# Attention and routed experts on one core: values as products of 64 rows without zeros, and x of four batches held back

## The chip, the cores and the metric

The kernel runs on one core of a Trainium2 chip. The metric is the device time of one execution in microseconds (us); lower is better. PE is TensorE's matmul, PEld its weight load, DVE is VectorE, ACT ScalarE, POOL GpSimd, and SP the engine that issues most of the plain transfers.

## The reference

```python
def _attn_ref(q, k, v, g_norm):              # (8, 8, 576, 64) each, g_norm (64,)
    kv = np.einsum('bhsd,bhse->bhde', k, v)
    out = np.einsum('bhsd,bhde->bhse', q, kv)
    rms = np.sqrt(np.mean(out * out, axis=-1, keepdims=True) + 1e-06)
    return out / rms * g_norm

# x = attention's output as (4608, 512)
def _moe_ref(x, w_skip, w_gate, w1, w2):     # 8 experts: w1 (8, 512, 1024), w2 (8, 1024, 512)
    do_compute = x @ w_skip > 0
    xc = x[do_compute]
    logits = xc @ w_gate
    e_idx = np.argmax(logits, axis=1)
    probs = np.exp(logits - logits.max(-1, keepdims=True))
    probs /= probs.sum(-1, keepdims=True) + 1e-09
    gate_w = probs[np.arange(len(xc)), e_idx]
    for e in range(E):
        mask = e_idx == e
        h = np.maximum(xc[mask] @ w1[e], 0.0)
        y[mask] = gate_w[mask, None] * (h @ w2[e])
    out = x.copy()
    out[do_compute] = xc + y
```

Everything is in fp32.

## The kernel before

Two stages follow each other: attention (to about 127 us of the profiled span), then the eight experts on rows gathered by an indirect transfer.

**Attention** works batch by batch, with eight heads of 64 each. Two heads share an operand: `w` numbers the two head pairs of a half, `u` the two halves of the heads, and `r` or `a` the two heads or rows of a pair, so that a head fills 64 of the 128 rows. For each batch six parts make the state, the product of k and v:

- `state` (L343), in thirds: 64x64 products of k and v into `sum_ps`; after the last third ACT copies the sums into `kvd` (L350).
- `state_t` (L357): the state turned, into `kvT_ps`, and copied by ACT (L360).
- `state_m` (L366): the turned state times the gate weights. The result gives nine more columns per head, so that a product of q with the state yields the gate logits beside the values; ACT copies them to both ends of the state (L369).
- `state_s` (L375, L379): the rows of the two heads of a pair swapped, through `sw_ps`, and copied by ACT.

`kvd` is a ring of five tiles (`KVD = 5`). In the kernel before, a tile is a block diagonal of 128 rows: each half of the rows holds its own state and zeros beside it, written once by memsets (L316: tile 0 by DVE, the others by POOL). Its values are then products over all 128 rows with 146 columns that move:

```python
nc.tensor.matmul(out=ps[:, w, 0:2 * PK].rearrange("p (r k) -> p r k", r=2)[:, :, cols],
                 lhsT=qT[:, w, a, :], rhs=kvds[b % KVD][:, u, w, :, cols], ...)
```

The work is cut into 36 **units**: four for each batch (two quarters `i` times two halves `u`), and after every four batches two more, with `i` None, for the ninth row of each group (L458, 64x64 products). Batch b of the first four starts at unit 4b, batches 4 to 7 at units 18, 22, 26 and 30. A unit takes these steps, pipelined over the loop `for n in range(NU + 2)`: `turn` (L414, four transposes of q, and ACT's copy L417), `values` (L450, into a tile of `ps_o`, of which there are two, or late in the stage into `sum_ps`), ACT's squares (L464), `squares` (DVE's sum L472), `root` (ACT L479), `norm` (DVE's reciprocal L486 and the product `xl` L489, which empties the PSUM tile), and `finish` (POOL: the logits L506 to L514 and the product with g_norm into `xb`, L524).

The order on every engine is the order of the program[...]. Jobs for a later step are put in lists by `at(step, part, job)` and called at the parts "early", "pe", "dve" and "end" of that step. The state of batch b is made at the steps from six before its first unit on. At the end of its first unit `load_kv(b + 3)` is issued on SP (there are three buffers each for k and v), and two steps later `load_q(b + 2)` (two buffers). When a batch's `xb` is done, one half is stored by POOL's queue (L545) and the other, one step later, by SP's (L546).

The gating runs beside it in three groups (`ends = [12, 22, 36]`): from steps 12 and 22 on, a few DVE operations a step choose, rank and number the rows of the tokens so far. In the second group the order of the experts is found, the weights of the first one are loaded on SP (L302, L305, into the tiles `w1` and `w2` of `wpool_a`), and `early` gathers the first 128 rows of that expert from the batches 0 to 4 already stored (L756).

**Experts.** The first expert's layers are plain products (L972, L983), the other seven use products of half-size blocks and sums (L1051). The weights of each next expert are loaded while the one before runs.

## Time and profile before

| What | Value |
|---|---|
| Median of 3 runs | 403.25 us (401.68 to 403.75) |
| Profiled execution, its own time | 404.02 us |
| Its span | 402.2 us |
| Busy: PE, PEld, DVE, ACT, POOL | 371.8, 323.1, 254.4, 144.7, 123.5 us |
| Mean granted clock | 0.956 |
| Read from and written to memory | 66.80 and 14.48 MB |
| Last xl of the attention stage, start | 128.4 us |
| First product of the first expert (L972), start | 129.25 us |

Times in the profile count from the start of the span. A line such as L450 is a line of the kernel before; the changed kernel has other numbers for the same operations. An fp32 matmul of the program is two matmul instructions with a weight load each, while a transpose is one. Matmuls are pipelined, so that the time from the first start of a group to the first start of the next says more than the durations. Busy shares are of the whole span; what a stage is bound by is read from a table of windows.

### The profile page before, as it was taken

The numbers are of one execution on the slowest core, as the hardware profiler recorded it, in microseconds if no ns is written. First come the engines' busy times: TensorE is split into PE (matmuls) and PEld (weight loads), VectorE is DVE, ScalarE is ACT, GpSimd is POOL, SyncE is SP. The second block draws the span as 40 slices with busy tenths as digits, with TensorE's granted clock in tenths as the row PEclk, the third lists the DMA queues.
The fourth block names the chain that finished last, engine by engine and source line by source line (L and its number), as shares of the span: only waits on it lengthen the run. The fifth ranks groups of instructions, "written<-read, shape, count | busy, mean of one in ns | idle before, by whom it ended". The sixth has DMA issues, their size and how long they took to land.

```text
span 402.2 us, 9616 instructions
## 1 busy us (share of the span) xinstructions
PE 371.8 (92%) x3849; PEld 323.1 (80%) x3849; DVE 254.4 (63%) x621; ACT 144.7 (36%) x384; POOL 123.5 (31%) x192
## 2 busy tenths in 40 slices
PE   7789999999874989999999999999999999999992
PEld 4678988888763948859978987998988988989981
DVE  2233568899976761366674775766766776868811
ACT  1365786676743212203510440430430430431410
POOL 7024577665658243111204301231221111212001
PEclk9599999999986898999999999999999999999997
DMA  8999999898595882346252651752752752711001
GB/s 299 394 391 392 316 391 400 250 364 222 169 406 134 255 322 73 102 161 224 73 203 67 250 193 55 260 182 94 257 188 90 258 177 96 255 55 38 16 2 49
DMA packets 31287, 81.70 MB, mean 203 GB/s; under 512 B 1850, under 2 KB 1858, under 8 KB 31236
## 3 DMA queue, kind: packets, MB, share of 16 engines
q1 hardware_dynamic: 26688, 66.59, 47.9%
q0 software_dynamic: 4528, 14.41, 11.0%
q8 instruction: 32, 0.52, 0.5%
q14 instruction: 19, 0.16, 0.1%
q10 hardware_dynamic: 20, 0.02, 0.0%
HBM read 66.80 MB, written 14.48 MB: 202 GB/s over the span
## 4 chain that ended last, share of the span: by engine, by line
PE 71%; DVE 10%; issue 8%; ACT 4%; DMA 3%; POOL 2%; ACTq 0%; DVEq 0%; POOLq 0%
PE bank L1051 40%; PE bank L983 8%; PE bank L972 6%; PE o_ps L450 4%; DVE xl L489 3%; PE sum_ps L343 3%; PE q_ps L414 3%; PE bank L953 2%; DMA xg<-out_dram,src 2%; DVE rs L472 1%; PE g_ps L357 1%; DMA xb<-in_g_norm_dram 1%; ACT qT L417 1%; PE g_ps L366 1%; ACT rs L479 1%
## 5 line engine op out<-in xcount | busy, mean ns | idle before, releaser
L1061 ACT COPY p<-bank 128x144 f32<-128x144 f32 (+4 forms) x70 | 20.9, 299 | 106.1 <-PE bank L1051 91.9
L1051 PE MATMUL bank<-xt,w 128*128 128x144 f32 (+3 forms) x336 | 56.5, 291 | 0.0
L1051 PEld LDWEIGHTS bank<-xt,w 128*128 128x128 f32 x336 | 47.8, 190 | 1.9 <-DVE bank L1055 1.2
L1055 DVE TENSOR_TENSOR bank<-bank,p 128x144 f32<-128x144 f32 (+4 forms) x70 | 23.8, 340 | 40.3 <-PE bank L1051 38.5
L450 PE MATMUL o_ps<-kvd,qT 128*128 128x146 f32 x240 | 36.9, 296 | 3.8 <-DVE xl L489 1.4
L1193 POOL DMA_INDIRECT out_dram<-xg,rows x16 | 16.2, 1011 | 77.8 <-DVE xg L1190 77.2
L524 POOL TENSOR_TENSOR xb<-xl,g_b 128x512 f32<-128x512 f32 x32 | 38.2, 1193 | 1.2 <-DMA out_dram<-xb 1.2
L1051 PE MATMUL bank<-xs,s 128*128 128x144 f32 (+3 forms) x224 | 37.4, 292 | 0.0
L450 PEld LDWEIGHTS o_ps<-kvd,qT 128*128 128x128 f32 x240 | 32.5, 193 | 5.7 <-DVE xl L489 2.4
L983 PE MATMUL bank<-w,ht 128*32 128x128 f32 (+2 forms) x448 | 36.6, 322 | 0.0
L943 POOL DMA_INDIRECT xg<-out_dram,src x15 | 15.9, 1057 | 56.3 <-PE bank L1051 36.2
L1193 POOL DMA_INDIRECT out_dram<-xg,arows x8 | 9.0, 1129 | 76.9 <-DVE xg L1190 76.6
L1051 PEld LDWEIGHTS bank<-xs,s 128*128 128x128 f32 x224 | 31.6, 190 | 1.0 <-ACT p L1061 0.3
L472 DVE TENSOR_REDUCE rs<-sq 128x8 f32<-128x512 f32 x36 | 24.4, 679 | 12.3 <-ACT sq L464 12.1
L983 PEld LDWEIGHTS bank<-w,ht 128*32 128x32 f32 (+2 forms) x448 | 20.4, 121 | 13.6 <-issue 10.9
L489 DVE TENSOR_TENSOR xl<-o_ps,rs 128x584 f32<-128x584 f32 x33 | 25.3, 767 | 4.4 <-PE g_ps L366 0.5
L1051 PE MATMUL bank<-w,ht 128*128 128x256 f32 x112 | 27.2, 386 | 0.0
L1051 PE MATMUL bank<-t,ht 128*128 128x256 f32 x112 | 27.1, 385 | 0.0
L343 PE MATMUL sum_ps<-v,k 64*64 64x64 f32 x1152 | 25.3, 229 | 1.4 <-issue 0.9
L972 PE MATMUL bank<-xt,w 128*128 128x128 f32 (+1 forms) x128 | 24.4, 360 | 1.5 <-ACT xt L956 1.0
L343 PEld LDWEIGHTS sum_ps<-v,k 64*64 64x64 f32 x1152 | 21.7, 140 | 4.5 <-issue 2.6
L1051 PE MATMUL bank<-t,hs 128*128 128x256 f32 x112 | 25.3, 379 | 0.0
(198 smaller groups left out, 697.0 us busy)
## 6 DMA issues: line engine op xcount, KB each, us to landing
w<-in_moe_w_dram SPq DMA_DIRECT2D x16, 2048.0 KB, 10.3
q<-in_q_dram SPq DMA_DIRECT2D x8, 1152.0 KB, 12.0
k<-in_k_dram SPq DMA_DIRECT2D x7, 1152.0 KB, 12.2
v<-in_v_dram SPq DMA_DIRECT2D x7, 1152.0 KB, 14.7
out_dram<-xb SPq DMA_DIRECT2D x8, 512.0 KB, 8.1
out_dram<-xb POOLq DMA_DIRECT2D x8, 512.0 KB, 7.5
k<-in_k_dram SPq DMA_DIRECT2D x2, 576.0 KB, 4.8
v<-in_v_dram SPq DMA_DIRECT2D x2, 576.0 KB, 6.8
```

The lines of the kernel that those rows point to most:

```text
L343: nc.tensor.matmul(out=sum_ps[w * 64:(w + 1) * 64, a, u, :], lhsT=kt[r, 2 * u + w, c, :], rhs=vt[r, 2 * u + w, c, :], start=(c == 0), stop ...
L450: nc.tensor.matmul(out=ps[:, w, 0:2 * PK].rearrange("p (r k) -> p r k", r=2)[:, :, cols], lhsT=qT[:, w, a, :], rhs=kvds[b % KVD][:, u, w, ...
L472: nc.vector.tensor_reduce(out=rs[:, :, :], in_=sq[:, :, :, :].rearrange("p x y (a d) -> p x (y a) d", a=2), axis=AX.X, op=ALU.add)
L489: nc.vector.tensor_tensor(out=xl[:, :, :, :].rearrange("p x y (a k) -> p x (y a) k", a=2), in0=ps[:, :, 0:2 * PK].rearrange("p x (h k) -> ...
L524: late.append(lambda: nc.gpsimd.tensor_tensor(out=xb[:, :, 4 * u * D:(4 * u + 4) * D].rearrange("p r (w x) -> p r w x", w=2), in0=xl[:, :, ...
L943: nc.gpsimd.indirect_dma_start(out=x_of(xg, off, m), out_offset=None, in_=cut_rows(m)[:, :], in_offset=bass.IndirectOffsetOnAxis(ap=idx[:, ...
L972: nc.tensor.matmul(out=hps[:, cols], lhsT=w_sb[r][0][:, dc, f * P:(f + 1) * P], rhs=xt[:, dc, cols], start=(dc == 0), stop=(dc == DC - 1))
L983: nc.tensor.matmul(out=yps[q * m:(q + 1) * m, 0:n], lhsT=ht[:, f, off:off + m], rhs=w_sb[r][1][:, f, q * n:(q + 1) * n], start=(f == 0), s ...
L1051: nc.tensor.matmul(out=out, lhsT=lhsT(i), rhs=rhs(i), start=start and i == 0, stop=i == k - 1, skip_group_check=True)
L1055: nc.vector.tensor_tensor(out=to, in0=x, in1=y, op=ALU.add)
L1061: nc.scalar.copy(out=t, in_=x)
L1193: ins = nc.gpsimd.indirect_dma_start(out=cut_rows(m)[:, :], out_offset=bass.IndirectOffsetOnAxis(ap=rows[:, col:col + 1], axis=0), in_=x, ...
```

## The change

Four things are done together.

1. `kvd` loses its zeros: a tile is `[P, 2, 2, PK]`, the own state and the swapped one, and no memset is left. Values become products of 64 rows: for each `w` and `a`, one for each half `r` of the rows, with 128 columns of weights and 73 columns that move, and the two halves write to different PSUM banks.
2. ACT's copies in `state`, `state_m` and `state_s`, two of 64 partitions each, become one of 128. `state_t` uses two transposes of 128x128 where it had four matmuls with the identity; `state_m` has four matmuls with 64 columns of weights where it had two with 128.
3. x of batches 0 to 3 is written into the room of the tiles `w1` (batches 0, 1) and `w2` (2, 3) of the first expert's weights, and not stored when done. Both halves are stored later by SP's queue, one batch at the end of each of the steps 21 to 24. Batches 4 to 7 are stored as before.
4. `load_kv(b + 3)` is issued at the end of step n - 3, where it was step n, but not before step 3 (batch 0's stays at step 0).

```diff
-        t = kvd_pool.tile([P, 2, 2, 2, PK], FP32, name=f"kvd{i}")
-        for r in range(2):
-            (nc.vector if i < 1 else nc.gpsimd).memset(t[r * 64:(r + 1) * 64, :, :, 1 - r, :], 0.0)
-        kvds.append(t)
+        kvds.append(kvd_pool.tile([P, 2, 2, PK], FP32, name=f"kvd{i}"))
...
-        for w in range(2):
-            nc.scalar.copy(out=own(b, w)[:, :, G:G + 2 * D].rearrange("p u (a d) -> p a u d", a=2),
-                           in_=sum_ps[w * 64:(w + 1) * 64, :, :, :])
+        nc.scalar.copy(
+            out=kvds[b % KVD][:, 0, :, G:G + 2 * D].rearrange("p u (a d) -> p a u d", a=2), in_=sum_ps)
...
     def state_t(b):
         for u in range(2):
-            for w in range(2):
-                r = slice(w * 64, (w + 1) * 64)
-                nc.tensor.matmul(out=kvT_ps[:, u, r], lhsT=kvds[b % KVD][:, u, w, w, G:G + 2 * D],
-                                 rhs=ident[:, r], start=True, stop=True)
+            nc.tensor.transpose(out=kvT_ps[:, u, :], in_=kvds[b % KVD][:, 0, u, G:G + 2 * D],
+                                identity=ident[:, :])
...
     def state_m(b):
...
-            nc.tensor.matmul(out=lg_ps[:, u, :, :, :], lhsT=kvT[:, u, :], rhs=gw_b[:, u, :, :, :],
-                             start=True, stop=True)
-        for w in range(2):
-            nc.scalar.copy(out=ends_of(own(b, w)), in_=lg_ps[w * 64:(w + 1) * 64, :, :, w, :])
+            for w in range(2):
+                r = slice(w * 64, (w + 1) * 64)
+                nc.tensor.matmul(out=lg_ps[r, u, :, :], lhsT=kvT[:, u, r], rhs=gw_b[:, u, :, w, :],
+                                 start=True, stop=True, skip_group_check=True)
+        nc.scalar.copy(out=ends_of(kvds[b % KVD][:, 0, :, :]), in_=lg_ps)
...
     def state_s(b):
...
-        for w in range(2):
-            o = slice((1 - w) * 64, (2 - w) * 64)
-            nc.scalar.copy(out=kvds[b % KVD][o, :, w, 1 - w, :],
-                           in_=sw_ps[o, :].rearrange("p (u k) -> p u k", u=2))
+        nc.scalar.copy(out=kvds[b % KVD][:, 1, :, :].rearrange("p u k -> p (u k)"), in_=sw_ps)
...
     def values(n):
...
-                if i is not None:
-                    nc.tensor.matmul(
-                        out=ps[:, w, 0:2 * PK].rearrange("p (r k) -> p r k", r=2)[:, :, cols],
-                        lhsT=qT[:, w, a, :], rhs=kvds[b % KVD][:, u, w, :, cols],
-                        start=True, stop=True, skip_group_check=True)
-                    continue
...
+                for r in range(2):
+                    rows, to = slice(r * 64, (r + 1) * 64), slice(w * PK + a * KD, w * PK + (a + 1) * KD)
+                    if i is not None:
+                        nc.tensor.matmul(out=ps[:, r, to], lhsT=qT[rows, w, a, :],
+                                         rhs=kvds[b % KVD][rows, w ^ r, u, cols],
+                                         start=True, stop=True, skip_group_check=True)
+                        continue
...
+    HELD = 4
+    stages, held_rows = {}, {}
+
+    def kept(b):
+
+        if b % 2 == 0:
+            shape, tag = ([P, DC, F], "w1") if b < 2 else ([P, FC, DM], "w2")
+            stages[b // 2] = wpool_a.tile(shape, FP32, tag=tag, name=tag)
+        flat = stages[b // 2][:, :, :].rearrange("p c f -> p (c f)")
+        n = NQ * 2 * DM
+        return flat[:, b % 2 * n:(b % 2 + 1) * n].rearrange("p (i r d) -> p i r d", i=NQ, r=2)
+
+    def store_held(b):
+        for hf in range(2):
+            rows, xb = held_rows.pop((b, hf))
+            nc.sync.dma_start(out=rows, in_=xb)
...
-                xbs[b, 0] = xb_pool.tile([P, NQ, 2, DM], FP32, tag="xb", name="xb")
+                xbs[b, 0] = kept(b) if b < HELD else \
+                    xb_pool.tile([P, NQ, 2, DM], FP32, tag="xb", name="xb")[:, :, :, :]
...
+            if b < HELD:
+                for hf in range(2):
+                    held_rows[b, hf] = (rows[hf], xb[hf * 64:(hf + 1) * 64, :, :, :]
+                                        .rearrange("p i r d -> p i (r d)"))
+                return None
...
-        at(n, "end", lambda b=b: load_kv(b + 3))
+        at(max(n - 3, 3 if b else 0), "end", lambda b=b: load_kv(b + 3))
...
+    for b in range(HELD):
+        at(starts[5] - 1 + b, "end", lambda b=b: store_held(b))
```

More of the change, by code (lines that the diff above doesn't have):

```diff
@@ L313 @@
     for i in range(KVD):
-        t = kvd_pool.tile([P, 2, 2, 2, PK], FP32, name=f"kvd{i}")
-        for r in range(2):
-            (nc.vector if i < 1 else nc.gpsimd).memset(t[r * 64:(r + 1) * 64, :, :, 1 - r, :], 0.0)
-        kvds.append(t)
-    def own(b, w):
-        return kvds[b % KVD][w * 64:(w + 1) * 64, :, w, w, :]
+        kvds.append(kvd_pool.tile([P, 2, 2, PK], FP32, name=f"kvd{i}"))
     sum_all = ps_kv.tile([P, 2, 512], FP32, name="sum_ps")
@@ L326 @@
     kvT_ps = g_ps[:, 0:2 * P].rearrange("p (u x) -> p u x", u=2)
-    lg_ps = g_ps[:, 2 * PK:2 * PK + 8 * G].rearrange("p (u a w g) -> p u a w g", u=2, a=2, w=2)
+    lg_ps = g_ps[:, 2 * PK:2 * PK + 4 * G].rearrange("p (u a g) -> p u a g", u=2, a=2)
     def ends_of(x):
@@ L374, in state_s @@
             r, o = slice(w * 64, (w + 1) * 64), slice((1 - w) * 64, (2 - w) * 64)
-            nc.tensor.matmul(out=sw_ps[o, :], lhsT=ident[r, r], rhs=own(b, w), start=True, stop=True,
-                             skip_group_check=True)
-        for w in range(2):
-            o = slice((1 - w) * 64, (2 - w) * 64)
-            nc.scalar.copy(out=kvds[b % KVD][o, :, w, 1 - w, :],
-                           in_=sw_ps[o, :].rearrange("p (u k) -> p u k", u=2))
+            nc.tensor.matmul(out=sw_ps[o, :], lhsT=ident[r, r],
+                             rhs=kvds[b % KVD][r, 0, :, :].rearrange("p u k -> p (u k)"),
+                             start=True, stop=True, skip_group_check=True)
+        nc.scalar.copy(out=kvds[b % KVD][:, 1, :, :].rearrange("p u k -> p (u k)"), in_=sw_ps)
     units = []
@@ L448, in values @@
                 cols = slice(a * KD, (a + 1) * KD)
-                if i is not None:
-                    nc.tensor.matmul(
-                        out=ps[:, w, 0:2 * PK].rearrange("p (r k) -> p r k", r=2)[:, :, cols],
-                        lhsT=qT[:, w, a, :], rhs=kvds[b % KVD][:, u, w, :, cols],
-                        start=True, stop=True, skip_group_check=True)
-                    continue
-                for hf in range(2):
-                    for r in range(2):
-                        rows, to = slice(r * 64, (r + 1) * 64), slice(hf * 64, (hf + 1) * 64)
-                        nc.tensor.matmul(
-                            out=ps[to, r, w * PK + a * KD:w * PK + (a + 1) * KD],
-                            lhsT=qT[rows, w, hf, a * 64:(a + 1) * 64],
-                            rhs=kvds[(4 * b + 2 * hf + r) % KVD][rows, u, w, r, cols],
-                            start=True, stop=True, skip_group_check=True)
+                for r in range(2):
[3 more added lines that the diff above has]
+                                         rhs=kvds[b % KVD][rows, w ^ r, u, cols],
+                                         start=True, stop=True, skip_group_check=True)
+                        continue
+                    for hf in range(2):
+                        nc.tensor.matmul(out=ps[hf * 64:(hf + 1) * 64, r, to],
+                                         lhsT=qT[rows, w, hf, a * 64:(a + 1) * 64],
+                                         rhs=kvds[(4 * b + 2 * hf + r) % KVD][rows, w ^ r, u, cols],
+                                         start=True, stop=True, skip_group_check=True)
         sq = att_pool.tile([P, 2, 2, 2 * D], FP32, tag="sq", name="sq", bufs=2)
@@ L511, in finish @@
                                     in1=lp[:, 1, :, :, :], op=ALU.add)
-            both = lp[:, 0, :, :, :] if i is not None else \
-                lp[:, 0, :, :, :].rearrange("p r w g -> p w r g")
-            nc.gpsimd.tensor_tensor(out=lgs[g][:, t0:t0 + 2, :], in0=both[:, 0, :, :],
-                                    in1=both[:, 1, :, :], op=ALU.add)
+            nc.gpsimd.tensor_tensor(out=lgs[g][:, t0:t0 + 2, :], in0=lp[:, 0, :, 0, :],
+                                    in1=lp[:, 0, :, 1, :], op=ALU.add)
         if i is None:
@@ L525, in finish @@
             out=xb[:, :, 4 * u * D:(4 * u + 4) * D].rearrange("p r (w x) -> p r w x", w=2),
-            in0=xl[:, :, :, G:G + 2 * D] if i is None else
-            xl[:, :, :, G:G + 2 * D].rearrange("p w r x -> p r w x"),
+            in0=xl[:, :, :, G:G + 2 * D],
             in1=g_b[:, :, :].rearrange("p a d -> p (a d)").unsqueeze(1).unsqueeze(1)
@@ L544, in finish @@
             rows = rows.rearrange("p (i hf r) d -> hf p i (r d)", hf=2, r=2)
+            if b < HELD:
+                for hf in range(2):
+                    held_rows[b, hf] = (rows[hf], xb[hf * 64:(hf + 1) * 64, :, :, :]
+                                        .rearrange("p i r d -> p i (r d)"))
+                return None
             nc.gpsimd.dma_start(out=rows[0], in_=xb[0:64, :, :, :].rearrange("p i r d -> p i (r d)"))
```

## The prediction

> **What bounds the kernel now.** I read the stages first. In this table of windows each row has the stretch, its length, the busy time of PE, of its weight loads, of DVE, ACT and POOL, the granted clock, the DMA share and GB/s.

> ```profile
> core 0: us, PE busy (x) PEld busy (x) DVE busy (x) ACT busy (x) POOL busy (x), PEclk, DMA share, GB/s
> 13.00:26.00 13.00, 12.38 (x148) 10.36 (x148) 0.87 (x3) 5.92 (x13) 0.00 (x0) 0.65 1.05 393
> 26.00:40.00 14.00, 12.14 (x253) 10.17 (x251) 6.26 (x12) 7.87 (x21) 6.52 (x12) 1.00 1.05 389
> 40.00:60.00 20.00, 19.82 (x323) 17.98 (x321) 11.90 (x23) 15.54 (x41) 12.50 (x22) 1.00 1.01 353
> 60.00:80.00 20.00, 18.48 (x425) 16.69 (x421) 16.78 (x36) 12.69 (x33) 13.76 (x25) 1.00 0.96 328
> 80.00:100.00 20.00, 19.25 (x373) 17.37 (x372) 18.52 (x38) 13.43 (x35) 11.75 (x21) 1.00 0.91 296
> 100.00:115.00 15.00, 11.05 (x144) 9.57 (x143) 14.08 (x33) 9.05 (x23) 7.83 (x15) 0.97 0.69 242
> 170.00:402.00 232.00, 223.41 (x1661) 195.53 (x1659) 150.79 (x361) 62.54 (x180) 41.23 (x40) 0.99 0.42 142
> ```

> The change lies in the attention stage, which ends near 127 us. Up to 60 us PE sets the pace: 19.82 of 20 us busy, DVE 11.90. From 80 to 115 DVE has nearly no room (18.52 of 20, 14.08 of 15); its own timeline is gapless there but for 0.39 us at 89.6. Between lies a mixed stretch. The experts after 127 us are bound by PE and not edited, so what the attention stage gains or loses moves the end one for one.

> DMA looks full to 60 us, but PE hardly waits for it: loads run ahead. In the waits of SP's queue the stores stand in front of loads, and by the timeline k and v still land 6 to 11 us before their first product (v7, issued at 74.25, lands by some 88 at v's median of 14.1 us; first used at 93.94). Sooner loads alone are worth nothing.

> Then PE's timeline (start, length, engine, line, operation, count):

> ```profile
> 51.01 1.17 PE L450 MATMUL o_ps<-kvd,qT 128*128 128x146 f32 x8
> 52.01 1.00 PE L357 MATMUL g_ps<-ident,kvd 128*128 128x64 f32 x8
> 52.85 0.61 PE L414 MATMUL q_ps<-ident,q 128*128 128x128 f32 x4
> ...
> 60.48 0.38 PE L433 MATMUL o_ps<-ident,q 128*128 128x128 f32 x2
> 60.70 1.17 PE L450 MATMUL o_ps<-kvd,qT 128*128 128x146 f32 x8
> 61.80 0.93 PE L343 MATMUL sum_ps<-v,k 64*64 64x64 f32 x48
> 62.66 0.66 PE L414 MATMUL q_ps<-ident,q 128*128 128x128 f32 x4
> ...
> 68.34 0.74 PE L458 MATMUL o_ps<-kvd,q 64*64 64x73 f32 x32
> 69.01 0.64 PE L366 MATMUL g_ps<-gw_b,kvT 128*128 128x36 f32 x4
> ```

> Price from start to next start: the values of a unit (L450) 1.00 us, 125 ns for each of 8 instructions; the turned state (L357) 0.84, or 105 ns each though only 64 columns move, so its weight loads set it; two fp32 transposes (L433) 0.22. A 64x64 run of 48 (L343) takes 0.86.

> Last the prologue:

> ```profile
> 11.74 0.55 DVE L316 MEMSET kvd<- 64x584 f32 x1
> 12.46 0.55 DVE L316 MEMSET kvd<- 64x584 f32 x1 [0.18 <-issue]
> 13.13 1.78 PEld L357 LDWEIGHTS g_ps<-ident,kvd 128*128 128x128 f32 x8 [1.86 <-ACT kvd L350]
> 13.16 1.94 PE L357 MATMUL g_ps<-ident,kvd 128*128 128x64 f32 x8 [1.70 <-DVE kvd L316]
> ```

> PE stands 1.70 us until the zeros of kvd 0 are written, then works at the low clock.

> [...] inside L343's 48, (0.93-0.21)/47 = 15 ns each, four quadrants together; entering costs 0.09 (L366 to L343 takes 0.46 us, to L414 0.36), leaving 0.12 (0.86-48x0.0153). [...] serial, L357 would need the load and the product, yet the whole takes 105 ns; in L343 the quadrants overlap too. No 64x128 fp32 tile is in the trace of before.

> **The change, part by part.**

> *Values.* Eight instructions of 128 rows become 16 of 64 rows, weights 128 columns, 73 columns moving, two row groups, each into its own bank. Product time per instruction is half of 125 ns, 63. Bounds: if only products count and the groups run together, 8 x 63 = 0.50 us; [...] I take 0.86, since L357 shows loads as the limit and L343 shows loads of four quadrants at once. That is 0.14 less than now. Against it stand the modes: by the program order, changes of mode on PE in this stage go from 55 to 99. 44 x 0.1 us = 4.4 us over 36 units, 0.12 a unit. Together about nothing, -0.02 a unit.

> *State.* L357's four matmuls (8 instructions, 0.84 us) become two transposes (0.22 to 0.25): -0.6 a batch. L366's 4 instructions (0.37) become 8 with 64 weight columns and 18 moving, in two column groups: 0.2 to 0.45, I take no difference. The swap products (L375) stay. On ACT each pair of half copies becomes one: -0.37 (L350), -0.20 (L369), -0.41 (L379), about 1 us a batch; ACT is not the bound, so mostly nothing, 0.3 us for waits like the 0.29 us for L379 at 36.98 and the 0.91 at 110.06.

> *Prologue.* No memsets on DVE; the transposes of batch 0 wait for one copy, 11.52+0.37 = 11.9 in place of 13.16: -1.2 us. At the low clock L357's 1.94 us becomes half of L414's four (1.04): -1.4. Sum -2.6. But the fast clock arrives only at 22.05 (L343's 48 take 0.93 there). If it comes at the same moment, the work pulled ahead of it runs at half speed: -1.3. I take -2.0. The 5 us of memsets on POOL hide nothing and cost nothing.

> *Stores and loads.* Four of POOL's store issues (0.65 us each) go; POOL has idle time, so nothing. SP loses the waits for POOL's xb ahead of four loads and gets eight issues (0.6 us each) from step 21 on. Behind them on SP stand the store of batch 4, the load of q 7, later the weights of expert 0. By the order of SP the first six issues come straight after q 6 (80.4 us), 3.1 MB; at 395 GB/s they are done in 8 us after q 6's 3, by 92, when q 7 is issued now (91.94) behind a store that waits for POOL. q 7 is used at 106.07. The weights, issued at 104 and first used at 129, must now wait for stores that have landed by 98 or so: at least 10 us of cover. The early gather (118.26) reads batches 0 to 4 and finds them stored. Price 0; if the cover were gone, some us. k and v go three steps sooner: 0, since they are early already.

> *Sum.* PE's -0.6 a batch counts while PE is the bound, some four batches to 80 us: -2.4, of which I drop 0.4 for the units that wait for DVE after 60 us (DVE has 3.2 us idle from 60 to 80). Values -0.02 x 20 units = -0.4, taken as 0. ACT -0.3, prologue -2.0. From 80 us on DVE's work is the same and carries the shift unchanged. Sum -4.3 us. The profiled execution took 404.02 us (span 402.2 and 1.8 around it), giving 399.7; it stands 0.8 above the median of 403.25, so against that 399.0.

> **The rivals.**

> *Slower: the weight loads of row tiles lie bare.* [...] +0.5 a unit over my sum. Some 30 units pay it, +15, less 2 that DVE hides from 80 us on; with -4.3 that is +9, 412. For it: [...] that no such tile was seen. Against it: L343 and L357. It decides from +0.2 us a unit over 20 units, which eats the 4.3. [...]

> *Faster still: the loads do not count.* Values at 0.50 us and 0.12 for the modes save 0.36 a unit: 4.3 over the 12 units before 60 us, and DVE's idle time lets through about 1.5 more: 393.2. Against it: L357's 105 ns.

> *Nothing.* The change does what it says, but [...] DVE swallows what comes after 40 us, and only the prologue's 1.3 is left: 402.

> *A transfer turns up late.* q 7 behind the held stores, or the expert's weights behind them: up to 3 us lost, 402. SP's order speaks against it.

> **How the numbers follow.** About 0.5% (2 us) is what a measurement of this kernel can tell from no change. My forecast has 0.54 (396 to 401), still faster 0.07, nothing or a late transfer 0.17, bare weight loads or queued ones 0.22. Some of the forecast's own spread lies within 2 us of no change, and of the third case a part falls beyond on the slow side. So faster 0.59, same 0.16, slower 0.25. Predicted 399.0. The range goes from just short of the fast rival, 394, to just short of the slow one's middle, 411; my forecast's own is 396 to 401.

> **What would show it.** Right: the values' group with twice the count and 0.85 to 1.0 us from first to next start; transposes of state at 0.22; first state transposes near 12 us; the first expert's products some 4 us before 129.25; DVE gapless from 76 to 112. Wrong: over 1.2 us a unit on the values, DVE with gaps after 80 us, or PE waiting for q after step 28.

## The result: slower by 0.6%, and the profile after

| | before | after |
|---|---|---|
| Median | 402.96 us (20 runs) | 405.75 us (20 runs) |
| After / before | | 1.0061 [1.0037, 1.0084] |
| Lowest and highest | 401.24, 407.06 us | 401.62, 412.64 us |
| Profiled execution, its own time | 404.02 us | 402.66 us |
| Its span, mean granted clock | 402.2 us, 0.956 | 400.7 us, 0.944 |

The ratios, here and below, leave disturbed runs out, so they can differ a little from the quotient of two medians.

The profiled execution of after is 3.1 us below its median, that of before 1.1 us above. The one trace therefore ends 1.5 us earlier though the kernel is slower, and what costs the time has to be looked for in something that differs from run to run. The stages of after, in the same columns as before:

```profile
core 0: us, PE busy (x) PEld busy (x) DVE busy (x) ACT busy (x) POOL busy (x), PEclk, DMA share, GB/s
13.00:26.00 13.00, 11.16 (x180) 8.42 (x180) 2.39 (x5) 6.74 (x15) 1.02 (x2) 0.80 1.05 391
26.00:40.00 14.00, 12.11 (x278) 9.77 (x276) 5.59 (x11) 6.47 (x16) 5.86 (x13) 1.00 1.05 391
40.00:60.00 20.00, 19.52 (x401) 16.35 (x403) 13.08 (x25) 13.50 (x36) 12.74 (x23) 1.00 1.05 388
60.00:80.00 20.00, 18.38 (x473) 15.96 (x466) 15.98 (x35) 11.50 (x29) 12.07 (x21) 0.91 0.59 204
80.00:100.00 20.00, 17.75 (x442) 15.17 (x437) 18.50 (x42) 11.29 (x28) 10.68 (x19) 1.00 0.97 337
100.00:115.00 15.00, 12.09 (x160) 10.11 (x150) 12.99 (x32) 7.71 (x20) 9.36 (x17) 0.84 0.94 335
115.00:127.00 12.00, 9.02 (x112) 7.67 (x110) 7.65 (x15) 5.11 (x12) 7.29 (x14) 0.50 0.65 230
170.00:402.00 232.00, 222.29 (x1660) 195.12 (x1658) 149.94 (x359) 61.89 (x177) 40.23 (x40) 0.99 0.41 141
```

The column to read is the clock: 0.91, 0.84 and 0.50 in three stretches where before had 1.00, 0.97 and, in the stretch from 115 to 127 us, this:

```profile
115.00:127.00 12.00, 7.06 (x97) 6.34 (x95) 8.10 (x18) 5.37 (x13) 9.65 (x18) 0.78 0.75 263
```

In after the clock is at half from 65.9 to 69.3 and from 110.2 to 134.1 us; in before, in this part, from 114.2 to 117.6 and from 124.4 to 134.7.

PE's timeline has the edited operations. L441 are the values (L450 before), L347 the turned state (L357), L358 its gate product (L366), L336 the 64x64 sums (L343), L446 the ninth rows (L458).

```profile
49.96 0.44 PE L347 MATMUL g_ps<-ident,kvd 128*128 128x128 f32 x2
50.23 0.38 PE L403 MATMUL q_ps<-ident,q 128*128 128x128 f32 x2
50.97 0.44 PE L403 MATMUL q_ps<-ident,q 128*128 128x128 f32 x2 [0.35 <-issue]
51.34 1.12 PE L441 MATMUL o_ps<-kvd,qT 64*128 64x73 f32 x16
52.38 0.41 PE L358 MATMUL g_ps<-gw_b,kvT 128*64 128x18 f32 x8
...
61.17 1.12 PE L441 MATMUL o_ps<-kvd,qT 64*128 64x73 f32 x16
62.22 0.93 PE L336 MATMUL sum_ps<-v,k 64*64 64x64 f32 x48
63.99 1.12 PE L441 MATMUL o_ps<-kvd,qT 64*128 64x73 f32 x16 [0.84 <-DVE xl L493]
65.03 0.44 PE L347 MATMUL g_ps<-ident,kvd 128*128 128x128 f32 x2
65.93 1.25 PE L446 MATMUL o_ps<-kvd,q 64*64 64x73 f32 x32 [0.46 <-DVE xl L493]
67.11 0.62 PE L358 MATMUL g_ps<-gw_b,kvT 128*64 128x18 f32 x8
67.66 1.56 PE L336 MATMUL sum_ps<-v,k 64*64 64x64 f32 x48
```

The values of a unit take 1.05 us from first start to next (61.17 to 62.22), 66 ns for each of 16, though one of them lasts 289 ns by the page (L441): their times overlap, as L450's 296 ns did in before with starts 125 ns apart. The state's two transposes take 0.27 (49.96 to 50.23). Then PE waits twice for DVE's `xl`, 0.84 and 0.46 us; behind that the same 48 products that took 0.93 us at 62.22 take 1.56.

And the prologue, the start of the chain in after:

```profile
10.44 2.20 PE L336 MATMUL sum_ps<-v,k 64*64 64x64 f32 x72 [0.84 <-DMA v<-in_v_dram]
12.70 0.38 ACT L342 COPY kvd<-sum_ps 128x256 f32<-128x256 f32 x1 [4.73 <-PE sum_ps L336]
13.12 0.69 PE L347 MATMUL g_ps<-ident,kvd 128*128 128x128 f32 x2 [0.49 <-ACT kvd L342]
```

No memset stands before the transposes, but v landed 1.2 us later in this execution (10.44 against 9.26), so they start at 13.12, not at 11.9. The first values still start at 18.35 against 19.96. Part of that is chance: they take 1.12 us here, at full clock, and in e0_again, the same kernel, they start at 18.63 and take 1.99.

### The profile page after: what moved, and what is told of

Its sections match the earlier page's. It is cut to its first block, busy times and chain, and to the rows that moved or that the text cites. A ratio compares the mean times of both kernels' runs of the same rounds, so it can differ in the third digit from the quotient of the medians.

```text
span 400.7 us, 10049 instructions
## 1 busy us (share of the span) xinstructions
PE 371.0 (93%) x4089; PEld 318.4 (79%) x4089; DVE 252.0 (63%) x619; ACT 136.5 (34%) x360; POOL 116.1 (29%) x180
## 4 chain that ended last, share of the span: by engine, by line
PE 72%; DVE 10%; DMA 7%; issue 7%; ACT 2%; POOL 1%; DVEq 0%; POOLq 0%; SPq 0%; ACTq 0%
PE bank L1061 42%; PE bank L993 8%; PE bank L982 6%; PE o_ps L441 5%; DMA v<-in_v_dram 4%; DVE xl L493 3%; PE sum_ps L336 3%; PE q_ps L403 3%; PE bank L963 2%; DMA xg<-out_dram,src 2%; DVE rs L459 2%; DVE oha_k L631 2%; DMA k<-in_k_dram 1%; PE g_ps L657 1%; PE o_ps L422 1%
## 5 line engine op out<-in xcount | busy, mean ns | idle before, releaser
L1061 PEld LDWEIGHTS bank<-xt,w 128*128 128x128 f32 x336 | 47.8, 190 | 1.9 <-DVE bank L1065 1.4
L441 PE MATMUL o_ps<-kvd,qT 64*128 64x73 f32 x480 | 35.9, 289 | 3.0 <-DVE xl L493 2.7
L441 PEld LDWEIGHTS o_ps<-kvd,qT 64*128 64x128 f32 x480 | 31.4, 196 | 8.7 <-issue 4.2
L993 PE MATMUL bank<-w,ht 128*32 128x128 f32 (+2 forms) x448 | 36.6, 322 | 0.0
L993 PEld LDWEIGHTS bank<-w,ht 128*32 128x32 f32 (+2 forms) x448 | 20.4, 121 | 13.6 <-issue 10.9
L336 PE MATMUL sum_ps<-v,k 64*64 64x64 f32 x1152 | 27.0, 237 | 3.8 <-issue 2.4
L336 PEld LDWEIGHTS sum_ps<-v,k 64*64 64x64 f32 x1152 | 23.2, 147 | 6.2 <-issue 4.6
L982 PEld LDWEIGHTS bank<-xt,w 128*128 128x128 f32 x128 | 23.6, 233 | 2.5 <-ACT xt L966 1.3
L406 ACT COPY qT<-q_ps 128x512 f32<-128x512 f32 x32 | 18.8, 586 | 19.6 <-PE q_ps L403 19.5
```

What stands on the lines that cost most here:

```text
L336: nc.tensor.matmul(out=sum_ps[w * 64:(w + 1) * 64, a, u, :], lhsT=kt[r, 2 * u + w, c, :], rhs=vt[r, 2 * u + w, c, :], start=(c == 0), stop ...
L406: nc.scalar.copy(out=qT[:, :, :, :].rearrange("p w a t -> p (w a t)"), in_=ps[:, :, :, :, :].rearrange("p w a h t -> p (w a h t)"))
L441: nc.tensor.matmul(out=ps[:, r, to], lhsT=qT[rows, w, a, :], rhs=kvds[b % KVD][rows, w ^ r, u, cols], start=True, stop=True, skip_group_ch ...
L982: nc.tensor.matmul(out=hps[:, cols], lhsT=w_sb[r][0][:, dc, f * P:(f + 1) * P], rhs=xt[:, dc, cols], start=(dc == 0), stop=(dc == DC - 1))
L993: nc.tensor.matmul(out=yps[q * m:(q + 1) * m, 0:n], lhsT=ht[:, f, off:off + m], rhs=w_sb[r][1][:, f, q * n:(q + 1) * n], start=(f == 0), s ...
L1061: nc.tensor.matmul(out=out, lhsT=lhsT(i), rhs=rhs(i), start=start and i == 0, stop=i == k - 1, skip_group_check=True)
```

## The experiments

The mean clock below is that of all runs of a kernel, not of its profiled one. The runs of before beside these experiments had 0.962 to 0.966 on every chip used. For a single run this mean is rough: a stretch without a record counts as full clock, and in the traces of e0_again, e3, e6, e9 and e10 the record starts only at 19.7 to 24.1 us, though the products before it took the longer times of the half clock (the values 1.99 us at 18.63 in e0_again, 1.12 at 23.50). Such a mean can be up to 0.02 too high, by an estimate from these traces. Between 25 and 127 us, which all 14 traces have on record, the clock is at half for 4.9 to 10.2 us in the kernels with values of 128 rows (before 6.0) and for 14.6 to 24.3 us in those with 64 (after 20.1).

| run | what it is | ratio to before | mean clock | runs below 0.945 |
|---|---|---|---|---|
| e0_again | after, again | 1.0107 [1.0045, 1.0168] | 0.937 | 4 of 6 |
| e1_values | after, without the held x | 1.0067 [1.0038, 1.0096] | 0.945 | 11 of 22 |
| e2_held | before, with the held x | 0.9991 [0.9960, 1.0022] | 0.962 | 0 of 14 |
| e3_xb3 | after, three buffers for xb | 1.0059 [1.0032, 1.0087] | 0.947 | 12 of 22 |
| e4_b64 | before, values of 64 rows only | 1.0076 [1.0038, 1.0115] | 0.947 | 6 of 12 |
| e5_quad | after, values of 64x64 | 1.0253 [1.0202, 1.0304] | 0.939 | 4 of 6 |
| e6_fill | after, with filler products | 1.0067 [1.0040, 1.0095] | 0.953 | 6 of 20 |
| e7_tmm | after, turned state by matmuls | 1.0155 [1.0096, 1.0214] | 0.945 | 2 of 6 |
| e8_memset | before, zeros of tile 0 by POOL | 0.9982 [0.9957, 1.0008] | 0.964 | 0 of 22 |
| e9_keep | e8, state turned by transposes | 1.0171 [1.0127, 1.0214] | 0.969 | 0 of 6 |
| e10_tiny | before, 256 tiny products more | 1.0160 [1.0116, 1.0204] | 0.966 | 0 of 6 |
| e11_both | e2 and e8 together | 0.9969 [0.9934, 1.0004] | 0.966 | 0 of 14 |

### Which part costs: e0, e1, e2, e3, e4

**e0_again** is after unchanged:

> The changed kernel once more, for a second profile and for the scatter of its times. Theory L (a late store): POOL's first xb of batch 7 waits 3 us or more for the store of batch 5, which SP issues behind expert 0's weights, and these wait for the last held store; ratio to before about 1.005. Theory C (the granted clock): the wait is not longer than the 1.25 us of before, and the low clock around 110 to 134 us costs PE 2 us or more. Theory I (instruction fetch): the idle stretches of PE that the profile puts down to issue sum to over 4 us before 128 us, where before has 1.5.

Slower again, by 1.1%, with the lowest mean clock of all; six runs give it a wide interval.

**e1_values** takes the held x and the earlier loads out of after:

```diff
-    HELD = 4
+    HELD = 0
...
-        at(max(n - 3, 3 if b else 0), "end", lambda b=b: load_kv(b + 3))
+        at(n, "end", lambda b=b: load_kv(b + 3))
```

> The values, state and copies of the change alone: no x is held and k and v are loaded at step n as before. Theory L: the store of batch 5 is issued as before, so the gain of some 2 to 4 us comes through: ratio 0.990 to 0.995. Theory C: less work on PE is what lowers the clock, so the loss stays: ratio 1.003 to 1.01. Theory I: as C, since the added instructions are all here.

**e2_held** is the other half: before with the parts 3 and 4 of the change, `kept` and `store_held` as in its diff.

```diff
+    HELD = 4
...
-                xbs[b, 0] = xb_pool.tile([P, NQ, 2, DM], FP32, tag="xb", name="xb")
+                xbs[b, 0] = kept(b) if b < HELD else \
+                    xb_pool.tile([P, NQ, 2, DM], FP32, tag="xb", name="xb")[:, :, :, :]
...
-        at(n, "end", lambda b=b: load_kv(b + 3))
+        at(max(n - 3, 3 if b else 0), "end", lambda b=b: load_kv(b + 3))
```

> The held x and the sooner loads alone, on the products of before. Theory L: 2 to 4 us lost, ratio 1.005 to 1.01, with POOL waiting 3 us or more at the first xb of batch 7. Theories C and I: no loss, ratio 0.998 to 1.002.

e1 has the whole loss, e2 none of it: the held x is neutral within 0.4%, and the loss is in the products and copies.

**e3_xb3.** After's trace showed one suspect in the stores (who waits for what: us in total, times, longest):

```profile
POOL xb L527 <- DMA out_dram<-xb: 3.7, 1, 3.7
```

POOL's first write for batch 7 waits 3.7 us for the store of batch 5, which stands behind the weights on SP; before, the same wait was 1.2 us. A third buffer takes the cause away:

```diff
-    xb_pool = attn.enter_context(tc.tile_pool(name="xb", bufs=2))
+    xb_pool = attn.enter_context(tc.tile_pool(name="xb", bufs=3))
```

> The changed kernel with three buffers for xb where it has two, so that the first xb of batch 7 waits for no store. Theory L: the attention stage ends some 2 us sooner than in the changed kernel and the ratio to before falls to 0.990 to 0.996. Theories C and I: no difference from the changed kernel, ratio 1.004 to 1.008.

The wait is gone from its trace, and the ratio is 1.0059 against after's 1.0061: the late store is not the cause.

**e4_b64** makes only the values narrow. The tiles keep their zeros, the state its four matmuls, ACT its half copies; two views in `finish` follow the new order in `ps`.

```diff
-                    nc.tensor.matmul(
-                        out=ps[:, w, 0:2 * PK].rearrange("p (r k) -> p r k", r=2)[:, :, cols],
-                        lhsT=qT[:, w, a, :], rhs=kvds[b % KVD][:, u, w, :, cols], ...)
+                    for r in range(2):
+                        rows = slice(r * 64, (r + 1) * 64)
+                        nc.tensor.matmul(
+                            out=ps[:, r, w * PK + a * KD:w * PK + (a + 1) * KD],
+                            lhsT=qT[rows, w, a, :], rhs=kvds[b % KVD][rows, u, w, r, cols], ...)
```

> The kernel before with one edit: the values as products of 64 rows, on the tiles with zeros; state, copies, memsets, stores and loads as before. Theory V (products of 64 rows let the clock drop): mean granted clock near 0.945 where before has 0.964, ratio 1.005 to 1.015. Theory T (the state's transposes in place of matmuls let it drop) or theory W (it is the smaller amount of work on PE): clock near 0.960 and a ratio of 0.998 to 1.004, since PE has as much to do as before.

1.0076 and a clock of 0.947: the narrow values alone bring the loss and the clock with it. After has the gains in the prologue and the state on top, and its interval overlaps e4's, so what came through of those gains is small.

### Why the clock falls: e5, e6, e7, e10

Over all kernels with values of 64 rows, after included, 55 of 114 runs had a mean clock below 0.945 (after itself 10 of 20, with 0.946 on average); over those with 128 rows, the runs of before beside these experiments included, none of 190. Within the 20 runs of after the time falls by 1.5 us for each 0.01 of clock; within the 128 of before by 1.2, but by 0.4 to 2.2 in the sets of runs that these come from. A fall of 0.018 (0.964 to 0.946) then is worth 2.1 to 2.7 us, an estimate about as large as the whole measured loss of 2.5 (0.61% of 403). It is not a shown price: a run in which PE stalls longer has both a longer time and a lower clock. With one slope for all kernels of a chip, e0, e1, e3 and e4 still stand 0.6 to 1.7 us above before at the same clock.

The clock in the traces is either 1.0 or 0.5, and changes only on a grid of 3.41 us: after's stretches at half clock above are one such step (65.9 to 69.3) and seven (110.2 to 134.1), before's one (114.2 to 117.6) and three (124.4 to 134.7). Two windows on that grid, each with the next, first of e4, then of before:

```profile
65.50:68.90 3.40, 2.73 (x46) 2.42 (x47) 2.92 (x8) 1.71 (x6) 2.12 (x6) 1.00 1.03 398
68.90:72.30 3.40, 3.40 (x84) 3.14 (x81) 2.73 (x5) 1.60 (x5) 2.04 (x5) 0.50 1.01 395
```

```profile
63.00:66.40 3.40, 2.50 (x60) 2.01 (x58) 3.26 (x7) 2.22 (x5) 1.69 (x4) 1.00 1.04 388
66.40:69.80 3.40, 3.40 (x64) 3.21 (x68) 2.96 (x7) 2.05 (x6) 3.14 (x6) 1.00 1.04 410
```

PE is busy 2.73 of 3.4 us in e4, and the clock halves; it is busy only 2.50 in before, and the clock stays. In these two, busy time alone does not decide. What differs, by an estimate of mine, is how much of the array works. I weighted each product by rows times columns of its tile (128x128 is 1), and its time by the columns that move: 0.84 ns each in fp32 (six products of 512 columns took 2.82 us and four 1.96 in after, L993 at 139.60 and 142.62, so 0.43 each; L450 has 125 ns for 146), half of that for bf16 (two of 512 took 0.44 us in e6, L401 at 76.56). Transposes count in full, since two of them took 0.22 us, 0.86 ns a column. By this estimate, e4's window has a share of 0.34, that of before 0.54. The 14 traces have 1,451 windows at full clock on the grid, 68 of them before a slow one. A limit of 0.34 on this share tells all but 4 whether the next window is slow, and in the six kernels with 128-row values (633 windows, 26 falls) all of them; the best limit on busy time fails in 19. Windows before a fall have at most 0.37, windows before none at least 0.34. The limit was found on these same traces, so its value is rough. So in these traces the falls go with the share of cells at work better than with busy time. The change also adds changes of mode on PE, from tiles of one shape to tiles of another (128*128 to 64*128, say), but they are not what marks a fall: from 20 to 127 us, in the kernels with narrow values, a window before a fall holds 1.4 of them on average, any other 3.7.

The same columns of q against the same state are worth twice as much in before: half of each 128-row product is multiplication by zeros. In this estimate the zeros count as work: e4 leaves them out and its clock falls (0.947), and a share without them tells the windows less well (its best limit fails in 8 in place of 4). From 24 to 108 us the mean share is 0.70 in before and e2, 0.52 in after, 0.50 in e4. In before's window above, 0.9 us of idle time leave the share over the limit; in e4's, 0.7 us push it under, and so do 1.3 us in after's, from 62.5 us on.

**e5_quad** narrows the values further:

```diff
+                        for hf in range(2):
+                            nc.tensor.matmul(out=ps[hf * 64:(hf + 1) * 64, r, to],
+                                             lhsT=qT[rows, w, a, hf * 64:(hf + 1) * 64],
+                                             rhs=kvds[b % KVD][rows, w ^ r, u, cols], ...)
```

> The changed kernel with its values as products of 64 rows and 64 columns, four at a time, as the units of the ninth rows have them: by their price of 0.67 us a unit PE has 0.38 us less a unit. Theory V: as many rows are idle, or more, clock at or below 0.945, and a ratio to before of 1.00 to 1.01. Theory I (instruction fetch): twice the instructions of the values, the idle time put down to issue rises by 3 us or more, ratio above 1.01. If neither, PE's saving before 60 us comes through: ratio 0.985 to 0.995.

2.5% slower, with a mean share of 0.44. PE's waits show a second cost (line, what it waited for, us in total, times, longest):

```profile
PE sum_ps L336 <- issue: 11.4, 6, 3.2
PE o_ps L442 <- issue: 4.7, 4, 1.8
...
PE q_ps L403 <- issue: 3.3, 1, 3.3
```

In 19.9 us from 20 to 127 nothing that the profile shows held PE back. In before these stalls are 1.15 us, in after 2.96. What they wait for is not shown. That it is instructions (theory I) stays a guess: after's trace has a queue for them (q8 on its page, 34 packets, 0.56 MB), with one of 16 KB about every 6 us from 24 to 104 us, but no run ties a stall to it.

**e6_fill** puts cells back to work: two wide products ahead of the transposes of q, overwritten by them.

```diff
+        for _ in range(2 if n >= 16 else 0):
+            nc.tensor.matmul(out=ps[:, :, :, :, :].rearrange("p w a h t -> p (w a h t)"),
+                             lhsT=ones[:, :], rhs=ones[:, :].unsqueeze(1).to_broadcast([P, 4, P]), ...)
```

> The changed kernel with two more bf16 products of 128 rows and 512 columns, which nothing reads, ahead of q's transposes from unit 16 on: some 0.43 us more for PE in each of 18 units. Theories V, T and W all say that this keeps the clock up: mean clock 0.955 or more, and the time falls below that of the changed kernel in spite of the added work, ratio to before 0.990 to 1.003. Theory I, or a loss that has nothing to do with the clock: 2 to 7 us longer than the changed kernel, ratio 1.01 to 1.02.

The clock rose by 0.007 over after's (0.953 to 0.946), in the direction that the theory of the clock has, if less than expected; the time did not fall below after's. The fillers may cost what they return. So this run speaks for the share of cells, and shows no price for the clock.

**e7_tmm** asks whether it is the transposes that let the clock fall, and turns the state of after by four 128-row matmuls:

```diff
-            nc.tensor.transpose(out=kvT_ps[:, u, :], in_=kvds[b % KVD][:, 0, u, G:G + 2 * D],
-                                identity=ident[:, :])
+            for w in range(2):
+                r = slice(w * 64, (w + 1) * 64)
+                nc.tensor.matmul(out=kvT_ps[:, u, r], lhsT=kvds[b % KVD][:, 0, u, G:G + 2 * D],
+                                 rhs=ident[:, r], start=True, stop=True)
```

> The changed kernel with the state turned by four matmuls of 128 rows as before, in place of two transposes. Theory T: the clock comes back to about 0.960 and the ratio to before falls to 0.992 to 1.000, the clock's gain being more than the 0.6 us a batch that it costs. Theory V: clock stays near 0.945, ratio 1.007 to 1.015. Theory W: between, clock near 0.950.

The clock did not come back (0.945), and the kernel is slower still. That theory falls.

**e10_tiny** separates the number of instructions from the work: before, with as many PE instructions more as the change adds (256 to 240), which hardly use the array.

```diff
+        for _ in range(8):
+            nc.tensor.matmul(out=ps[:, 0, 0, 0, 0:8], lhsT=ones[:, :], rhs=ones[:, 0:8], ...)
```

> The kernel before, with eight more bf16 products of 128x128 weights and 8 moving columns ahead of the transposes of q of each of 32 units, results overwritten: 256 more PE instructions, about as many as the change adds (240), and hardly any work of the array. If the clock falls because the array's cells do less work in a window, it stays near 0.96 here (0.955 to 0.967) and the time grows only by the products' own 0.2 to 0.4 us a unit where PE is the bound [...]: ratio 1.005 to 1.02. If the number of instructions brings the low clock, [...] it falls to 0.937 to 0.953 as in the kernels with values of 64 rows.

The mean clock is 0.966, and no run of six is below 0.963: the number of instructions alone does not bring the low clock. The kernel is 6.5 us slower all the same, but that is no price for the number of instructions, since the tiny products take PE's time themselves:

```profile
40.31 0.36 PE L412 MATMUL q_ps<-ones 128*128 128x8 bf16 x8
40.52 0.64 PE L417 MATMUL q_ps<-ident,q 128*128 128x128 f32 x4
```

That is 0.21 us a unit, 6.7 over the 32 units if nothing hides it. Beside it, stalls without a shown cause grow to 4.2 us from 20 to 127, and the window with the longest of them (1.83 us, share 0.28) is the only one before 115 us after which the clock falls. So this trace has 10.2 us at half clock between 25 and 127, more than before's 6.0 and less than the 14.6 or more of the kernels with narrow values.

### What of the change is worth keeping: e8, e9, e11

**e8_memset** is the part of the zeros in the prologue alone:

```diff
-            (nc.vector if i < 1 else nc.gpsimd).memset(t[r * 64:(r + 1) * 64, :, :, 1 - r, :], 0.0)
+            nc.gpsimd.memset(t[r * 64:(r + 1) * 64, :, :, 1 - r, :], 0.0)
```

> The kernel before, with the zeros of tile 0 of kvd written by POOL like the others, none by DVE: the prologue's share of the gain by itself, with the products of 128 rows kept. If the prologue's start carries through, the first transposes of the state wait for ACT's second half copy (12.3 us) in place of the memset (13.16): 0.9 us earlier, of which some is lost at the low clock: ratio 0.997 to 0.999. If the fast clock's arrival at 22 us sets the time, nothing: 0.999 to 1.001. Mean clock as before, 0.96.

0.9982, -0.7 us (-1.7 to +0.3): in the direction expected, not beyond the uncertainty. In its trace the first transposes start at 12.10 us in place of 13.16 and wait for ACT's copy.

**e9_keep** adds the turned state by two transposes, from a copy without zeros:

```diff
+        kvc = att_pool.tile([P, 2, 2 * D], FP32, tag="kvc", name="kvc", bufs=1)
+        nc.scalar.copy(out=kvc[:, :, :].rearrange("p u (a d) -> p a u d", a=2), in_=sum_ps)
...
-                nc.tensor.matmul(out=kvT_ps[:, u, r], lhsT=kvds[b % KVD][:, u, w, w, G:G + 2 * D],
-                                 rhs=ident[:, r], start=True, stop=True)
+            nc.tensor.transpose(out=kvT_ps[:, u, :], in_=kvc[:, u, :], identity=ident[:, :])
...
+            nc.scalar.copy(out=own(b, w)[:, :, G:G + 2 * D], in_=kvc[w * 64:(w + 1) * 64, :, :])
```

> The kernel before, with tile 0's zeros by POOL, and the state turned by two transposes from a copy of its own without zeros (one ACT copy of 128 partitions, the two half copies into kvd behind it): what of the change takes work off PE without making it narrow in the values. If the loss came from the narrow values' clock, this keeps the clock near 0.96 and gets the change's own gains: 0.6 us a batch on PE for some four batches and 1 us of the prologue, -2 to -3.5 us, ratio 0.991 to 0.996. If any saving of PE time in this stage is eaten by DVE or by the clock, 0.998 to 1.002.

A plain miss: no low clock (0.969, and in the trace 4.9 us at half clock between 25 and 127), the transposes at 0.22 us in place of 0.84, and 1.7% slower. From its waits on PE between 26 and 127 us:

```profile
PE o_ps L451 <- DVE xl L490: 3.8, 5, 1.2
...
PE sum_ps L344 <- issue: 2.0, 2, 1.4
PE q_ps L415 <- issue: 1.4, 1, 1.4
PE q_ps L415 <- DMA q<-in_q_dram: 0.8, 1, 0.8
PE q_ps L415 <- ACT qT L418: 0.8, 2, 0.6
```

The waits for `xl` before the values were 1.4 us in before, those for q's transfer none. The values start 1.9 us early at unit 0, 0.9 early at unit 4 and 0.9 late at unit 15. So PE time saved in the first 60 us went in part into waits for DVE, ACT and q. ACT's extra copy per batch may have a part in it, and how large a part isn't settled, nor the rest of the 6.9 us: the trace is 2.4 us longer than before's.

**e11_both** joins e2 and e8, both on products of 128 rows. On e2 it is one line:

```diff
-            (nc.vector if i < 1 else nc.gpsimd).memset(t[r * 64:(r + 1) * 64, :, :, 1 - r, :], 0.0)
+            nc.gpsimd.memset(t[r * 64:(r + 1) * 64, :, :, 1 - r, :], 0.0)
```

> The two neutral or better parts put together on the products of 128 rows: x of four batches held back with the earlier loads (0.9991 of before by itself) and the zeros of tile 0 written by POOL (0.9982 by itself). If both gains are real and add up: ratio 0.997, 0.995 to 0.9995, mean clock 0.96. If they were chance, 0.999 to 1.001.

402.64 us against 404.79 for before on the same chip, 0.9969 with an interval that just takes in 1. It is the best version found; that it beats before is likely and not shown.

## Why the prediction was wrong

I forecast 399.0 us, 4.3 below the median of 403.25 that I had; measured was 405.75, and by the ratio 2.5 us slower than before.

**Right in kind and nearly in size.** Values: 0.86 + 0.12 a unit predicted, 1.05 measured against 1.00 before. By an estimate from before's trace, with the 105 ns of L357 for a load and 63 ns, half of L450's 125, for a product, the loads of the two groups side by side take 0.84 a unit, load and product in turn 1.34, all 16 loads one after another 1.68, the products alone 0.50. So it is neither bare weight loads nor free ones. The modes and the loads together were sized 0.07 too low, about 1.4 us over the 20 units that were counted. State: -0.6 a batch on PE came (0.84 to 0.27). Stores and loads: e2 puts them at nothing, as predicted, though the store of batch 5 came late by a way I had not named.

**Wrong: the sum carried PE's savings to the end one for one.** "What the attention stage gains or loses moves the end one for one" is true of the end of the stage, but not of each step in it. In after's trace the values start 1.6 us early at unit 0 and only 2.1 early at unit 22 (84.62 against 86.69), where the state was to bring 2.0 more and brought 0.5. The stalls without a shown cause took 1.8 us more than before between 20 and 127. Of the prologue's 2.0, e8 has only the part of the zeros, which I put at 1.2, and measures 0.7 (-0.3 to 1.7); e9, with the state's 0.6 a batch, ends later and not sooner.

**Wrong: the granted clock was left as it was.** The working used it only in the prologue. No step priced that 64-row products occupy half of the array's rows (tiles of 64*128 in after's timeline, 128*128 in before's), and none of the rivals had it; the slower rival named bare weight loads, which the trace denies (1.05 us a unit against the 1.34 above). The narrow values alone cost 0.8%, or 3.1 us (e4); by the slopes above the clock would be 2.1 to 2.7 of them. In after's own trace the lead shrinks at the end, from 2.1 us at L752's products (111.81 against 113.95) to 1.3 at the first expert's (127.99 against 129.25), in a stretch where the clock is 0.50 in place of 0.78. This execution met only one slow window between 20 and 108 us. e4's met two slow stretches of two windows each, with a clock of 0.83 from 60 to 80 and from 80 to 100; it took 411.9 us, one of the longest of e4's twelve:

```profile
60.00:80.00 20.00, 19.33 (x463) 17.06 (x453) 15.15 (x31) 11.19 (x28) 11.51 (x22) 0.83 0.93 328
80.00:100.00 20.00, 18.48 (x292) 16.05 (x290) 13.21 (x28) 11.77 (x30) 10.64 (x19) 0.83 0.63 213
```

DVE does 13.21 us of work in the second stretch where before did 18.52: in that execution the stage that DVE was to carry unchanged had become PE's again (18.48 of 20 us busy, at the lower clock). So of the forecast's 4.3 us and the loss of 2.5, 6.8 us apart, the clock explains some 2.1 to 2.7 and the values about 1.4 by these estimates, neither of them a measured price; the rest is gains that didn't pass through, and how it divides between stalls of PE and waits for DVE and ACT isn't settled.

## What to carry to other kernels

Here cutting the multiplications by zero out of the values saved no time (1.05 us a unit against 1.00) and went with a lower clock (0.946 on average against 0.964); before narrowing a tile, compare the windows of the trace that hold a stall and ask whether they would still keep the clock. Short instructions are to be priced too: eight tiny products took 0.21 us of PE in e10. And when one profiled execution ends earlier while the median is later, look at what varies from run to run, the granted clock first.
